# V stored by token of a block, then by block, in a block-sparse attention and feed-forward kernel

## The chip, the cores and the metric

The kernel is one program on one core of a Trainium2 chip. The core has a matrix engine (PE, with its weight loads shown as PEld), a vector engine (DVE), an activation engine (ACT), a general engine (POOL), and a queue engine (SP) that issues transfers. Transfers between DRAM and the on-chip memory (128 partitions) are carried out by 16 DMA engines. The metric is the device time of one execution in microseconds, median of several runs; lower is better.

## The reference

Attention with a block mask over 4 batches, 8 heads, 768 tokens and 64 values per head, and then a feed-forward layer with a softplus between two matrix products:

```python
block, n_blocks, n_rand = 32, 24, 3
mask = np.abs(blk_i - blk_j) <= 1
mask = mask | (blk_i == 0) | (blk_j == 0) | (blk_i == n_blocks - 1) | (blk_j == n_blocks - 1)
for qb in range(n_blocks):
    for kb in sampled_blocks[qb]:
        mask[qb * block:(qb + 1) * block, kb * block:(kb + 1) * block] = True
scores = np.where(mask, q @ k.T / sqrt(64), -1e9)
attn = softmax(scores)                 # attn / (sum + 1e-9)
x = (attn @ v), heads side by side     # 3072 tokens x 512
h = x @ w_in                           # 512 x 2048
out = softplus(h) @ w_out              # 2048 x 512
...
```

So a block of 32 queries sees its own block, the two beside it, the first and the last block, and three sampled ones: eight slots of 32 keys. The first and the last block of queries see all 24 blocks.

## The kernel before

**Sets of query blocks.** The 24 query blocks of a batch are taken in six groups `g` of four, in the order 1, 2, ..., 23, 0. Each group is a set, and the last group of a batch (blocks 21 and 22, 23 and 0) makes two: first a whole set (blocks 23 and 0, which see all keys), then a set of two blocks. That gives 7 sets for a batch and 28 in all. A set is worked off in two units (half of the heads each).

**The values of a set** lie in one of two buffers `vbuf` (`vg` in the trace), 128 partitions x 2 x 4 x 512 floats, that the sets use in turn. For a set of four blocks, `vd[0:96, 0, i]` holds the neighbour rows of block `i` (three blocks of 32 tokens on 96 partitions), `vd[96:128, 0, i]` and `vd[96:128, 1, i]` the first and the last block, and `vd[0:96, 1, i]` the three sampled blocks. `load_values(m)` loads them: one transfer from SP's queue for all neighbour rows (L549), transfers for the ends in the first two sets of a batch (L558, L561), and for each block a gather from POOL's queue with a table of row numbers (L567; L362 for the ends of the very first block). For a whole set three transfers (L542) bring all 768 rows of the batch.

**V in DRAM** is a table of 3072 rows (batch, then token) of 512 floats, 2 KB a row. So the rows of one block follow one another in DRAM, and the four neighbour rows that one partition takes (the same token of four blocks in a row) lie 64 KB apart. The pattern of L549 is written by `overlapping`:

```python
return bass.AP(at.tensor, at.offset, [pattern[0], [BLOCK * pattern[0][0], n], pattern[1]])
```

Its steps, outermost first, are 96 rows 2 KB apart, then `n` blocks, then the 512 floats of a row.

**The tables of row numbers** are made at the start: POOL writes the number of the token in its block on each partition (`io` L357, `first` L359), and DVE makes the row `block * 32 + token + batch * 768` of it (`ixf` L391, `ix` L396).

**What sets the order.** The work of the attention is cut into pieces (`pieces`: scores, values, transposes of a unit), and `attend` deals them out between the matrix products of the first feed-forward stage; between these `convert` runs the conversion of the weights (raw weights in at L148, converted ones parked in DRAM at L201). PE takes its instructions in that fixed order. SP's queue is in program order too. `value_piece` calls `values(n)` and, after the second unit of set `m`, `load_values(m + 2)`, since the buffer is free from then on. So the load of a set is issued when the set two before it is done, and it has to be there when PE comes to the first values of its own set. The keys of a batch (`kT`, L431) are loaded anew at the end of each batch.

After the attention, from about 430 us of the trace, the second feed-forward stage runs; it loads no values.

Of the kernel before, what the change touches and what calls it, by code (L numbers as in the profile page):

```python
# [15 lines left out]
ALU = mybir.AluOpType  # L16
# [3 lines left out]
BLOCK = 32  # L20
# [30 lines left out]
def sparse_attention_ffn(  # L51
# [22 lines left out]
    nc = tc.nc  # L74
    B, NG, P, NP, NI, _ = q.shape
    NB = k.shape[2]
    S = NB * BLOCK
    LAST = NB - 1
    NA = NP // 2
    NT, DM = out.shape  # L80
    NF = w_in.shape[0]
    NC = DM // P
    D = DM // (2 * NP)
    SCALE = 1.0 / float(D) ** 0.5
    NS = 8
    NR = 3
    TB = GROUPS * P
    NTB = NT // TB
    NCH = S // P
# [245 lines left out]
    rf = ac.tile([P, NB, NR], F32, name="rf")  # L335
# [3 lines left out]
    io = ac.tile([NR * BLOCK, 1], I32, name="io")  # L339
    first = ac.tile([P, 1], I32, name="first")  # L340
    iof = ac.tile([NR * BLOCK, 1], F32, name="iof")
    ixf = ac.tile([NR * BLOCK, NB], F32, name="ixf")
    ix = ac.tile([NR * BLOCK, B, NB], I32, name="ix")
# [8 lines left out]
    for i in range(NI):  # L352
        nc.gpsimd.iota(
            iu[i * BLOCK : (i + 1) * BLOCK], pattern=[[NI, NG]], base=1 + i, channel_multiplier=0
        )
    for s in range(NR):
        nc.gpsimd.iota(io[s * BLOCK : (s + 1) * BLOCK], pattern=[[0, 1]], base=0, channel_multiplier=1)  # L357
    for rows in (slice(0, NR * BLOCK), slice(NR * BLOCK, P)):
        nc.gpsimd.iota(first[rows], pattern=[[0, 1]], base=0, channel_multiplier=1)  # L359
    vbuf = [ac.tile([P, 2, NI, DM], F32, name=f"vg{n}") for n in range(2)]  # L360

    nc.gpsimd.indirect_dma_start(  # L362
        out=vbuf[0][:, 0, 0, :], out_offset=None, in_=v,
# [21 lines left out]
    def make_index():  # L385
        nc.vector.tensor_copy(out=iof, in_=io)
        nc.vector.tensor_copy(out=rf, in_=blk.rearrange("p (i s w) -> p i s w", s=NR, w=2)[:, :, :, 0])

        for s in range(NR):
            rows = slice(s * BLOCK, (s + 1) * BLOCK)  # L390
            nc.vector.tensor_scalar(  # L391
                out=ixf[rows], in0=rf[rows, :, s], scalar1=float(BLOCK), scalar2=iof[rows, 0:1],
                op0=ALU.mult, op1=ALU.add,
            )
        for b in range(B):
            nc.vector.tensor_scalar_add(out=ix[:, b], in0=ixf, scalar1=float(b * S))  # L396

    def make_mask():
        nc.vector.tensor_copy(out=iuf, in_=iu)
# [10 lines left out]
        nc.vector.tensor_single_scalar(out=hit, in_=tmp, scalar=1.0, op=ALU.is_le)  # L410
        for end in (0.0, float(LAST)):
            nc.vector.tensor_single_scalar(out=tmp, in_=rp, scalar=end, op=ALU.is_equal)
# [12 lines left out]
    kT, qc, vg = {}, {}, {}  # L425
# [7 lines left out]
    def load_kT(b, n, engine=nc.sync, parts=4):  # L433
        load_part(b, n * NB // parts, (n + 1) * NB // parts, engine)

    def overlapping(src, lo, n, rows):

        at = src[lo : lo + rows]
        pattern = [list(x) for x in at.ap]
        return bass.AP(at.tensor, at.offset, [pattern[0], [BLOCK * pattern[0][0], n], pattern[1]])  # L440

    def load_queries(m):
        if m >= len(order):
# [33 lines left out]
    def end_keys(m, copies):  # L477

        for copy, slot, blkno in zip(copies, (NR, 2 * NR + 1), (0, LAST)):
            copy(  # L480
# [4 lines left out]
    def gather_keys(m):  # L485
# [4 lines left out]
        def of_block(i):  # L490
# [15 lines left out]
            for s in range(NR):  # L506
                x = nc.s_assert_within(
                    eng.snap((r >> (16 * (i % 2) + 5 * s)) & 31), 0, LAST,
                    skip_runtime_bounds_check_because="a sampled block is one of the key blocks",
# [23 lines left out]
    def load_values(m):  # L533
        if m >= len(sets):
            return
        b, g, whole = sets[m]
        vd = vg[sets[m]] = vbuf[m % 2]
        if whole:
            rows = vd.rearrange("p c i f -> p (c i) f")
            for n in range(0, NCH, 2):  # L540
                lo = b * S + n * P
                nc.sync.dma_start(  # L542
                    out=rows[:, n : n + 2], in_=v[lo : lo + 2 * P].rearrange("(t p) f -> p t f", p=P)
                )
            return
        ni = NI if g < NG - 1 else 2

        i0 = 1 if m == 0 else 0
        nc.sync.dma_start(  # L549
            out=vd[0 : 3 * BLOCK, 0, i0:ni], in_=overlapping(v, b * S + (4 * g + i0) * BLOCK, ni - i0, 3 * BLOCK)  # L550
        )
        if g < 2:

            for c, lo in enumerate((b * S, (b + 1) * S - BLOCK)):
                i1 = i0 if c == 0 else 0
                if m < SPREAD:
                    if i1 == 0:
                        nc.sync.dma_start(out=vd[3 * BLOCK : P, c, 0], in_=v[lo : lo + BLOCK])  # L558
                    spread.append((vd[3 * BLOCK : P, c, 0:1], vd[3 * BLOCK : P, c, 1:]))
                    continue  # L560
                nc.sync.dma_start(  # L561
                    out=vd[3 * BLOCK : P, c, i1:],
                    in_=v[lo : lo + BLOCK].unsqueeze(1).to_broadcast([BLOCK, NI - i1, DM]),
                )

        def of_block(i):
            nc.gpsimd.indirect_dma_start(  # L567
                out=vd[0 : 3 * BLOCK, 1, i, :],
                out_offset=None,
                in_=v,  # L570
                in_offset=bass.IndirectOffsetOnAxis(ap=ix[:, b, 4 * g + 1 + i : 4 * g + 2 + i], axis=0),
            )

        value_work.extend((m, lambda i=i: of_block(i)) for i in range(ni))
# [6 lines left out]
    def scores(n):  # L581
        m, a = units[n]
        b, g, whole = sets[m]
        st = state[n]
        qd = qc[b, g]
        nmax = st["nmax"] = wk.tile([P, 2, 2], F32, tag="nmax", name=f"nmax{n}", bufs=4)
        st["pr"] = [wk.tile([P, S], F32, tag="pr", name=f"pr{n}_{r}", bufs=4) for r in range(2)]
        if not whole:
            gathered(key_work, place[b, g])
            kd = kg[place[b, g] % 2]  # L590
            ni = NI if g < NG - 1 else 2
            rows = slice(0, ni * BLOCK)
            ps = [ps_s.tile([P, 2, NS, BLOCK], F32, tag="s", name=f"s{n}_{r}") for r in range(2)]
            pr = [x[:, 0 : 2 * NS * BLOCK].rearrange("p (j s k) -> p j s k", j=2, s=NS) for x in st["pr"]]
            for j in range(2):
                p = 2 * a + j
                cols = slice(p * BLOCK, (p + 1) * BLOCK)
                for i in range(ni):
                    for r in range(2):
                        half = slice(64 * r, 64 * r + 64)  # L600
                        nc.tensor.matmul(  # L601
                            ps[r][32 * i : 32 * i + 32, j], qd[half, p, i, :], kd[half, i, :, cols],
                            start=True, stop=True,
                        )
            for r in range(2):
                for j in range(2):
                    nc.vector.tensor_tensor_reduce(  # L607
                        out=pr[r][rows, j], in0=ps[r][rows, j],
                        in1=mask[rows, g].unsqueeze(2).to_broadcast([ni * BLOCK, NS, BLOCK]),
                        scale=-SCALE, scalar=BIG, op0=ALU.add, op1=ALU.min,  # L610
                        accum_out=nmax[rows, r, j : j + 1],
                    )
            st["rows"] = ni * BLOCK
            st["chunks"] = 4
        else:

            pr = st["pr"]
            for t, (lo, hi) in enumerate(((0, NB // 2), (NB // 2, NB))):
                n_ = (hi - lo) * BLOCK
                ps = [ps_s.tile([P, 512], F32, tag="s", name=f"s{n}_{lo}_{r}") for r in range(2)]  # L620
                for o in range(2):
                    p = 2 * a + o
                    for r in range(2):
                        half = slice(64 * r, 64 * r + 64)
                        nc.tensor.matmul(  # L625
                            ps[r][64 * o : 64 * o + 64, 0:n_],
                            qd[half, p, 2:4, :].rearrange("p i q -> p (i q)"),
                            kT[b][half, lo:hi, p * BLOCK : (p + 1) * BLOCK],
                            start=True, stop=True,
                        )  # L630
                for r in range(2):
                    nc.vector.tensor_tensor_reduce(  # L632
                        out=pr[r][:, lo * BLOCK : hi * BLOCK], in0=ps[r][:, 0:n_],
                        in1=zero.to_broadcast([P, n_]),
                        scale=-SCALE, scalar=BIG, op0=ALU.add, op1=ALU.min, accum_out=nmax[:, r, t : t + 1],
                    )
            for r in range(2):
                nc.vector.tensor_tensor(out=nmax[:, r, 0:1], in0=nmax[:, r, 0:1], in1=nmax[:, r, 1:2], op=ALU.min)
            st["rows"] = P
            st["chunks"] = NCH  # L640
# [275 lines left out]
    for j in range(len(seq) + LEAD):  # L916
        if j >= SECOND:
            t, f = seq[j][1:] if j < len(seq) else (NTB, -1)
# [62 lines left out]
```

## Time and profile before

| | us |
|---|---|
| median of 3 runs | 831.7 |
| lowest, highest run | 827.58, 833.89 |
| span of the profiled execution (first to last instruction) | 812.1 |
| PE busy in the span | 781.7 |
| DVE, ACT, POOL busy in the span | 574.8, 489.6, 223.3 |

The profiled execution is one of its own; its time with what lies around its span is not among the three runs, and only its span is given. The median is 19.6 us above that span. Tables of the profile give the busy time of an engine, the granted clock of PE, the share of time for which the 16 DMA engines were busy on average, and the bytes that they moved per second. A packet is one piece that a DMA engine moves in one go. "Landing" is the time from issue to the arrival of the last byte. A transfer's KB are 1024 bytes, the MB of the queues are 10^6.

### The profile page before, as it was taken

What the parts mean: (1) busy time and instruction counts of PE and PEld (TensorE: products, weight loads), DVE (VectorE), ACT (ScalarE), POOL (GpSimd) and SP (SyncE); (2) the same over time, 40 slices, a digit from 0 to 9 for tenths busy, and PEclk for the clock granted to TensorE, in tenths of its full rate; (3) what the DMA queues carried; (4) which work ended last, traced back from release to release, by engine and by line L of the source; (5) the groups of instructions that cost most, each with busy time, mean ns of one, the idle gap of its engine ahead of it and who ended that gap; (6) DMA issues with size and microseconds to landing.
All of it is one profiled execution on the core that took longest, in us unless ns stands there. A gap on an engine that the chain in (4) does not pass through costs nothing.

```text
span 812.1 us, 21433 instructions
## 1 busy us (share of the span) xinstructions
PE 781.7 (96%) x8108; PEld 647.6 (80%) x8108; DVE 574.8 (71%) x1474; ACT 489.6 (60%) x1182; POOL 223.3 (27%) x389
## 2 busy tenths in 40 slices
PE   8878898999999999999999999999999999999997
PEld 8545676877677777778778988999988999988996
DVE  5778999876887777886655985656565656656564
ACT  5878785757767767767565764444444444444442
POOL 6864775635565436563000000000000000000000
PEclk9999898999999999999999999999999999999999
DMA  8899678687696777866425640304040312122021
GB/s 254 241 257 336 171 212 266 195 294 247 184 291 198 248 261 200 267 171 184 158 78 182 250 178 20 137 1 155 2 146 10 116 40 105 52 88 68 0 79 40
DMA packets 48408, 129.65 MB, mean 160 GB/s; under 512 B 5489, under 2 KB 5617, under 8 KB 46257
## 3 DMA queue, kind: packets, MB, share of 16 engines
q1 hardware_dynamic: 42304, 109.79, 42.3%
q0 software_dynamic: 5712, 17.57, 7.6%
q8 instruction: 64, 1.05, 0.5%
q10 hardware_dynamic: 288, 0.93, 0.3%
q14 instruction: 40, 0.32, 0.1%
HBM read 97.85 MB, written 30.41 MB: 158 GB/s over the span
## 4 chain that ended last, share of the span: by engine, by line
PE 82%; DVE 7%; ACT 6%; DMA 2%; issue 2%; POOL 0%; SPq 0%; ACTq 0%; DVEq 0%; POOLq 0%
PE o L295 11%; PE h L237 11%; PE o L297 10%; PE o L296 10%; PE h L238 10%; PE h L239 10%; PE s L601 5%; PE t L670 4%; PE x L700 4%; ACT pr L657 3%; PE warm L831 2%; DMA kT<-in_k_dram 1%; PE s L625 1%; DVE pr L607 1%; PE x L714 1%
## 5 line engine op out<-in xcount | busy, mean ns | idle before, releaser
L237 PE MATMUL h<-x,w 128*128 128x384 f32 x512 | 180.0, 352 | 0.4 <-DVE nmax L632 0.2
L238 PE MATMUL h<-x,w 128*128 128x384 f32 x512 | 173.7, 339 | 0.0
L239 PE MATMUL h<-x,w 128*128 128x384 f32 x512 | 173.1, 338 | 0.0
L250 DVE TENSOR_SCALAR u<-e 128x384 f32<-128x384 f32 x128 | 50.8, 397 | 155.8 <-ACT e L244 154.4
L295 PE MATMUL o<-w,gh 128*128 128x512 f32 x384 | 158.7, 413 | 0.0
L657 ACT ACTIVATE pr<-pr,nmax 128x256 f32<-128x256 f32 (+2 forms) x208 | 110.4, 532 | 74.6 <-DVE nmax L607 60.4
L297 PE MATMUL o<-w,gl 128*128 128x512 f32 x384 | 152.0, 396 | 1.2 <-issue 1.0
L296 PE MATMUL o<-w,gh 128*128 128x512 f32 x384 | 151.7, 395 | 0.0
L243 ACT ACTIVATE e<-h 128x384 f32<-128x384 f32 x128 | 62.4, 487 | 114.9 <-PE h L239 114.8
L267 ACT CAST gh<-u 128x384 fp32r<-128x384 f32 x128 | 65.6, 513 | 79.2 <-PE o L296 78.1
L237 PEld LDWEIGHTS h<-x,w 128*128 128x128 f32 x512 | 96.6, 189 | 19.4 <-issue 11.2
L567 POOL DMA_INDIRECT vg<-in_v_dram,ix x88 | 90.3, 1027 | 65.9 <-PE x L700 39.1
L238 PEld LDWEIGHTS h<-x,w 128*128 128x128 f32 x512 | 96.8, 189 | 6.5 <-issue 2.2
L511 POOL COPY kg<-kT 128x128 f32 x252 | 86.0, 389 | 41.2 <-PE s L601 38.8
L239 PEld LDWEIGHTS h<-x,w 128*128 128x128 f32 x512 | 96.6, 189 | 0.0
L295 PEld LDWEIGHTS o<-w,gh 128*128 128x128 f32 x384 | 72.0, 188 | 19.9 <-issue 7.1
L297 PEld LDWEIGHTS o<-w,gl 128*128 128x128 f32 x384 | 72.1, 188 | 18.8 <-issue 1.5
L296 PEld LDWEIGHTS o<-w,gh 128*128 128x128 f32 x384 | 72.2, 188 | 10.3 <-issue 0.4
L607 DVE CUSTOM_DVE_ANT_1 pr<-s,mask 128x256 f32<-128x256 f32 (+1 forms) x192 | 69.6, 414 | 14.5 <-PE s L601 14.5
L258 ACT ACTIVATE u<-u 128x384 f32<-128x384 f32 x128 | 66.9, 523 | 15.4 <-DVE e L252 15.2
L263 DVE TENSOR_TENSOR u<-u,e 128x384 f32<-128x384 f32 x128 | 73.6, 575 | 3.0 <-ACT u L258 2.4
L273 DVE TENSOR_TENSOR gl<-u,gh 128x384 fp32r<-128x384 f32 x128 | 73.0, 570 | 2.8 <-ACT gh L267 2.8
(81 smaller groups left out, 1088.6 us busy)
## 6 DMA issues: line engine op xcount, KB each, us to landing
vg<-in_v_dram SPq DMA_DIRECT2D x19, 768.0 KB, 5.8
xD<-x SPq DMA_DIRECT2D x8, 1536.0 KB, 7.4
x<-xD SPq DMA_DIRECT2D x8, 1536.0 KB
raw<-in_w_in_dram SPq DMA_DIRECT2D x16, 512.0 KB, 9.3
raw<-in_w_out_dram SPq DMA_DIRECT2D x16, 512.0 KB, 8.3
qc<-in_q_dram SPq DMA_DIRECT2D x24, 256.0 KB, 6.9
vg<-in_v_dram SPq DMA_DIRECT2D x12, 512.0 KB, 7.4
yD<-os SPq DMA_DIRECT2D x24, 256.0 KB, 2.5
```

Source lines behind the costliest of these rows:

```text
L237: nc.tensor.matmul(ph, wh[:, cols], hi[:, c], start=(c == 0), stop=False)
L238: nc.tensor.matmul(ph, wh[:, cols], lo[:, c], start=False, stop=False)
L239: nc.tensor.matmul(ph, wl[:, cols], hi[:, c], start=False, stop=(c == NC - 1))
L263: nc.vector.tensor_tensor(out=l, in0=l, in1=e, op=ALU.add)
L273: nc.vector.tensor_tensor(out=gl, in0=l, in1=G[n].bitcast(F32), op=ALU.subtract)
L295: nc.tensor.matmul(po[m], gh[:, cols], wh, start=first, stop=False)
L296: nc.tensor.matmul(po[m], gh[:, cols], wl, start=False, stop=False)
L297: nc.tensor.matmul(po[m], gl[:, cols], wh, start=False, stop=last)
L511: copy(out=kd[:, i, 1 + NR + s, :], in_=kT[b][:, bass.ds(x, 1), :].rearrange("p n f -> p (n f)"))
L567: nc.gpsimd.indirect_dma_start(out=vd[0 : 3 * BLOCK, 1, i, :], out_offset=None, in_=v, in_offset=bass.IndirectOffsetOnAxis(ap=ix[:, b, 4 * ...
L607: nc.vector.tensor_tensor_reduce(out=pr[r][rows, j], in0=ps[r][rows, j], in1=mask[rows, g].unsqueeze(2).to_broadcast([ni * BLOCK, NS, BLOCK]),
L657: nc.scalar.activation(x, x, AF.Exp, bias=nmax[rows, r, j : j + 1], scale=-1.0, accum_out=rs[rows, h : h + 1])
```

## The change

V is stored by batch, then by token of a block (32), then by block, with 25 places for the 24 blocks of a token (the last one is padding): row `(batch * 32 + token) * 25 + block`. The same token of successive blocks now lies in successive rows. A new function `tokens` writes the patterns of all loads of V. The neighbour load takes, on 96 partitions, one run of 8 KB (four rows); the whole set is one transfer with a run of 12 KB (six rows) on each of 128 partitions. For that, partition `s * 32 + token` of a whole set takes blocks `6 s` to `6 s + 5`, and the keys of its scores are read in the same order (`keys`). The tables of row numbers follow the new rows: POOL's numbers step by 25 from partition to partition, and the factor 32 of DVE's is gone. `first` gets its base by block.

```diff
+    PITCH = v.shape[0] // (B * BLOCK)
...
-    for s in range(NR):
-        nc.gpsimd.iota(io[s * BLOCK : (s + 1) * BLOCK], pattern=[[0, 1]], base=0, channel_multiplier=1)
-    for rows in (slice(0, NR * BLOCK), slice(NR * BLOCK, P)):
-        nc.gpsimd.iota(first[rows], pattern=[[0, 1]], base=0, channel_multiplier=1)
+    for s in range(NR + 1):
+        at = slice(s * BLOCK, (s + 1) * BLOCK)
+        if s < NR:
+            nc.gpsimd.iota(io[at], pattern=[[0, 1]], base=0, channel_multiplier=PITCH)
+        nc.gpsimd.iota(first[at], pattern=[[0, 1]], base=s % NR, channel_multiplier=PITCH)
...
-                out=ixf[rows], in0=rf[rows, :, s], scalar1=float(BLOCK), scalar2=iof[rows, 0:1],
-                op0=ALU.mult, op1=ALU.add,
+                out=ixf[rows], in0=rf[rows, :, s], scalar1=iof[rows, 0:1], scalar2=None, op0=ALU.add
...
-            nc.vector.tensor_scalar_add(out=ix[:, b], in0=ixf, scalar1=float(b * S))
+            nc.vector.tensor_scalar_add(out=ix[:, b], in0=ixf, scalar1=float(b * BLOCK * PITCH))
...
-    def overlapping(src, lo, n, rows):
-        at = src[lo : lo + rows]
-        pattern = [list(x) for x in at.ap]
-        return bass.AP(at.tensor, at.offset, [pattern[0], [BLOCK * pattern[0][0], n], pattern[1]])
+    def tokens(b, lo, n, parts=1, step=0):
+        at = v[b * BLOCK * PITCH + lo : b * BLOCK * PITCH + lo + 1]
+        row, one = [list(x) for x in at.ap]
+        pattern = [[PITCH * row[0], BLOCK], [row[0], n], one]
+        return bass.AP(at.tensor, at.offset, ([[step * row[0], parts]] if parts > 1 else []) + pattern)
...
-            for n in range(0, NCH, 2):
-                lo = b * S + n * P
-                nc.sync.dma_start(
-                    out=rows[:, n : n + 2], in_=v[lo : lo + 2 * P].rearrange("(t p) f -> p t f", p=P)
-                )
+            nc.sync.dma_start(out=rows[:, 0:NCH], in_=tokens(b, 0, NCH, NI, NCH))
...
-        nc.sync.dma_start(
-            out=vd[0 : 3 * BLOCK, 0, i0:ni], in_=overlapping(v, b * S + (4 * g + i0) * BLOCK, ni - i0, 3 * BLOCK)
-        )
+        nc.sync.dma_start(out=vd[0 : 3 * BLOCK, 0, i0:ni], in_=tokens(b, 4 * g + i0, ni - i0, 3, 1))
...
-            for c, lo in enumerate((b * S, (b + 1) * S - BLOCK)):
+            for c, end in enumerate((0, LAST)):
+                rows_v = tokens(b, end, 1)
...
+            keys = kT[b].rearrange("p (s c) f -> p c s f", s=NI)
...
-                            kT[b][half, lo:hi, p * BLOCK : (p + 1) * BLOCK],
+                            keys[half, lo:hi, :, p * BLOCK : (p + 1) * BLOCK],
```

Two places show how the instructions stand. On SP's queue around the first whole set (`vg` are value buffers, `raw` weights, `qc` queries, `kT` keys, `xD` a result parked in DRAM; behind the names stand partitions x counts of the written side), before:

```order
L148 DMA raw_1223<-in_w_in_dram 128x512
L542 DMA vg_174<-in_v_dram 128x2x512 x3
L447 DMA qc_0_1275<-in_q_dram 128x512
L148 DMA raw_1332<-in_w_out_dram 128x512
L431 DMA kT_1436<-in_k_dram 128x768 x4
L148 DMA raw_1456<-in_w_out_dram 128x512
L549 DMA vg_173<-in_v_dram 96x2x512
```

and with the change:

```order
L149 DMA raw_1225<-in_w_in_dram 128x512
L542 DMA vg_176<-in_v_dram 128x1x3072
L449 DMA qc_0_1275<-in_q_dram 128x512
L149 DMA raw_1332<-in_w_out_dram 128x512
L432 DMA kT_1436<-in_k_dram 128x768 x4
L149 DMA raw_1456<-in_w_out_dram 128x512
L547 DMA vg_175<-in_v_dram 96x1x1024
```

The three transfers of the whole set have become one and the counts of a partition one run; nothing has changed its place in the queue.

On POOL at the start of the program, before (`io` and `first` are the numbers from which the row tables are made):

```order
L353 IOTA iu 32x6 x3
L357 IOTA io 32x1 x3
L359 IOTA first 96x1
L359 IOTA first 32x1
L362 DMA vg_173<-in_v_dram,first 128x512
L567 DMA vg_173<-in_v_dram,ix 96x512 x4
```

and with the change:

```order
L354 IOTA iu 32x6 x3
L360 IOTA io 32x1
L361 IOTA first 32x1
L360 IOTA io 32x1
L361 IOTA first 32x1
L360 IOTA io 32x1
L361 IOTA first 32x1 x2
L364 DMA vg_175<-in_v_dram,first 128x512
L564 DMA vg_175<-in_v_dram,ix 96x512 x4
```

Two more IOTA instructions stand ahead of the first gather. On PE, DVE and ACT every instruction stands where it stood.

More of the change, by code (lines that the diff above doesn't have):

```diff
@@ L557, in load_values @@
                     if i1 == 0:
-                        nc.sync.dma_start(out=vd[3 * BLOCK : P, c, 0], in_=v[lo : lo + BLOCK])
+                        nc.sync.dma_start(out=vd[3 * BLOCK : P, c, 0:1], in_=rows_v)
                     spread.append((vd[3 * BLOCK : P, c, 0:1], vd[3 * BLOCK : P, c, 1:]))
@@ L562, in load_values @@
                     out=vd[3 * BLOCK : P, c, i1:],
-                    in_=v[lo : lo + BLOCK].unsqueeze(1).to_broadcast([BLOCK, NI - i1, DM]),
+                    in_=rows_v.to_broadcast([BLOCK, NI - i1, DM]),
                 )
@@ L617, in scores @@
             pr = st["pr"]
-            for t, (lo, hi) in enumerate(((0, NB // 2), (NB // 2, NB))):
-                n_ = (hi - lo) * BLOCK
+            keys = kT[b].rearrange("p (s c) f -> p c s f", s=NI)
+            for t, (lo, hi) in enumerate(((0, NCH // 2), (NCH // 2, NCH))):
+                n_ = (hi - lo) * P
                 ps = [ps_s.tile([P, 512], F32, tag="s", name=f"s{n}_{lo}_{r}") for r in range(2)]
@@ L632, in scores @@
                     nc.vector.tensor_tensor_reduce(
-                        out=pr[r][:, lo * BLOCK : hi * BLOCK], in0=ps[r][:, 0:n_],
+                        out=pr[r][:, lo * P : hi * P], in0=ps[r][:, 0:n_],
                         in1=zero.to_broadcast([P, n_]),
@@ L963 @@
         "k": k.reshape(B, NP, 2, NB, BLOCK, D).transpose(0, 2, 5, 3, 1, 4).reshape(B, 2 * D, NB, NP * BLOCK),
-        "v": v.transpose(0, 2, 1, 3).reshape(B * S, H * D),
+        "v": _np.pad(
+            v.reshape(B, H, NB, BLOCK, D).transpose(0, 3, 2, 1, 4), ((0, 0), (0, 0), (0, 1), (0, 0), (0, 0))
+        ).reshape(-1, H * D),
         "blocks": inputs["sampled_blocks"],
```

## The prediction

> **What bounds the kernel now.** I read the page's engine table first, then the 40 slices, then the chain that ended last.
>
> ```profile
> PE 781.7 (96%) x8108; PEld 647.6 (80%) x8108; DVE 574.8 (71%) x1474; ACT 489.6 (60%) x1182; POOL 223.3 (27%) x389
> PEclk9999898999999999999999999999999999999999
> DMA  8899678687696777866425640304040312122021
> ...
> PE 82%; DVE 7%; ACT 6%; DMA 2%; issue 2%; POOL 0%; SPq 0%; ACTq 0%; DVEq 0%; POOLq 0%
> ```
>
> PE is busy for 96% of the span at nearly full clock, and 82% of the last chain is PE work. DMA waits hold 2% of the chain, about 16 us. But the DMA row has its 6 to 9 tenths in the first 21 slices, which are the attention. The change touches only transfers of this stretch, so I read it by windows (columns: busy time of PE, PEld, DVE, ACT, POOL with counts; granted clock, mean DMA share, GB/s), with two later windows as prices.
>
> ```profile
> 0.00:429.00 429.00, 402.79 (x6207) 306.87 (x6209) 333.13 (x980) 303.38 (x802) 223.30 (x389) 0.98 0.74 223
> 140.00:180.00 40.00, 40.00 (x645) 31.29 (x645) 31.63 (x93) 29.22 (x81) 20.18 (x31) 1.00 0.71 226
> 380.00:429.00 49.00, 48.79 (x688) 37.93 (x689) 29.63 (x95) 30.84 (x80) 2.31 (x3) 1.00 0.35 122
> 435.00:445.00 10.00, 10.00 (x52) 9.01 (x51) 5.78 (x12) 5.31 (x12) 0.00 (x0) 1.00 0.99 353
> 505.00:515.00 10.00, 10.00 (x51) 8.91 (x51) 4.96 (x11) 4.93 (x10) 0.00 (x0) 1.00 0.42 157
> ```
>
> In the 429 us of attention the average DMA engine is busy for 0.74 x 429 = 317 us, and while busy it moves 223 / (0.74 x 16) = 18.8 GB/s. The windows at 435 (rows of 2 KB, weights) and 505 (runs of 12 KB, one `x` load) give 22.3 and 23.4 GB/s for one engine with little beside it. So PE bounds the stretch, with some 110 us of slack on each DMA engine, as long as the sixteen share the load.
>
> How they share it can be counted on ACT's queue:
>
> ```profile
> q1 hardware_dynamic: 42304, 109.79, 42.3%
> ...
> q10 hardware_dynamic: 288, 0.93, 0.3%
> ...
> kT<-in_k_dram ACTq DMA_DIRECT2D x1, 832.0 KB, 10.2
> ...
> blk<-in_blocks_dram ACTq DMA_DIRECT2D x1, 72.0 KB, 5.6
> ```
>
> Two transfers of 128 runs each make 256 packets; the queue counts 288. The 32 more are sixteen closing packets for each, one for every engine that took part. A run of 6.5 KB (832 KB / 128) is one packet: the runs are moved as the pattern lists them and not cut again.
>
> **The change part by part.** First the loads from SP's queue, with the time from issue to landing in the last column:
>
> ```profile
> vg<-in_v_dram SPq DMA_DIRECT2D x19, 768.0 KB, 5.8
> ...
> vg<-in_v_dram SPq DMA_DIRECT2D x12, 512.0 KB, 7.4
> ...
> vg<-in_v_dram SPq DMA_DIRECT2D x4, 384.0 KB, 8.1
> ...
> vg<-in_v_dram SPq DMA_DIRECT2D x1, 576.0 KB
> ```
>
> The 24 neighbour loads are 19 x 768 + 4 x 384 + 576 = 16,704 KB, the four whole sets 12 x 512 = 6,144 KB: together 23.4 MB of the 95.7 MB (223 GB/s x 429 us) of the stretch.
>
> *Longer runs.* 2 KB becomes 8 or 12 KB. By the rows at 435 and 505 a busy engine goes from 22.3 to 23.4 GB/s, which for 23.4 / 16 = 1.46 MB an engine saves 3 us of engine time in the whole kernel. That is nearly nothing.
>
> *The outermost step.* Before, the source pattern of a neighbour load began with 96 rows, that of a whole part with 128; sixteen equal shares can be taken from either. Now the source begins with `[step * row, parts]`: 3 for a neighbour load, 4 for a whole set, while the written side still begins with 96 or 128 partitions. What has to be decided is whether a transfer is divided along the outermost step of its patterns. If so, only 3 or 4 shares come out, on three or four engines. No row shows a transfer whose outer count is under sixteen: those of the value loads and of ACT's queue are 32, 96 and 128. I take the division along the outermost step, since the packet count shows patterns executed as written, run by run, with nothing that cuts them anew.
>
> [...]
>
> The price: three engines carry 16,704 / 3 + 6,144 / 4 = 7,104 KB, or 7.27 MB, of values each; at 23.4 GB/s (the row for long runs) that is 311 us. Their sixteenth of before falls away: 1.46 MB at 18.8 GB/s, 78 us. So each of these engines has 317 - 78 + 311 = 550 us of work for a stretch of 429 us, 121 us too much. In the last 49 us nothing overflows: 0.35 x 49 = 17 us, plus 16 for a whole set and a half-size load, leave 16 us idle. That makes +137 us. Against it stands that the other traffic may run faster when thirteen engines have less to do: its 239 us at 18.8 GB/s are 202 us at the 22.3 of the row at 435, which takes off 37 us and gives +100. Between these I take the middle, **+118 us**.
>
> Does it reach PE? One period of two sets, on PE and on SP's queue (start, duration):
>
> ```profile
> 143.99 1.10 PE L700 MATMUL x<-vg,pt 128*32 128x64 f32 x64
> 151.96 1.10 PE L700 MATMUL x<-vg,pt 128*32 128x64 f32 x64
> 159.49 1.10 PE L700 MATMUL x<-vg,pt 128*32 128x64 f32 x64
> 167.46 1.10 PE L700 MATMUL x<-vg,pt 128*32 128x64 f32 x64
> ...
> 145.04 0.33 SPq L549 DMA_DIRECT2D vg<-in_v_dram  x1
> ...
> 160.54 0.33 SPq L549 DMA_DIRECT2D vg<-in_v_dram  x1
> ```
>
> A set takes 15.5 us. The load issued at 145.04, right behind the last values of its buffer, is needed at 167.46: 22.4 us of cover. A neighbour load on three engines takes 262 KB at 23.4 GB/s, 11.2 us instead of 2.6 us (49 KB at 18.8), so alone it would still be covered. But it isn't alone: by the row at 140 a period holds 0.71 x 15.5 = 11.0 us of other and own work, and 11.0 + 8.6 = 19.6 us don't fit into 15.5. The backlog grows with every set, and from then on PE waits at the first values (L700) of a set, with everything behind them in its fixed order, the feed-forward products too. SP's queue carries queries, weights and keys behind the value loads, so these come late as well. For a whole set the cover is the time from issue to need here:
>
> ```profile
> 62.07 1.51 SPq L542 DMA_DIRECT2D vg<-in_v_dram  x3
> ...
> 82.30 1.62 PE L714 MATMUL x<-vg,pt 128*64 128x64 f32 x48
> ```
>
> 20.2 us, against 16.8 us on four engines (393 KB) plus the other work of that time.
>
> *Three transfers into one* takes two issues of 0.5 us (1.51 / 3) off SP, hidden under its waits. *Gathers.* The rows of a gathered block lie 51,200 B apart instead of 2,048. The nearest row is the long strided key load above (128 runs, 12 KB apart in the table, 10.2 us for 832 KB, in the crowded start), which shows no penalty: I take 0, with the range left to hold a few us either way. *The start.*
>
> ```profile
> 2.00 0.47 POOL L357 IOTA io<- 32x1 int32 x3
> 2.54 0.30 POOL L359 IOTA first<- 96x1 int32 x2
> 3.13 1.13 POOL L362 DMA_INDIRECT vg<-in_v_dram,first  x1 [0.29 <-POOL first L359]
> 7.82 0.91 POOL L567 DMA_INDIRECT vg<-in_v_dram,ix  x1 [3.56 <-DVE ix L396]
> ```
>
> Two more IOTAs are 2 x 0.15 = 0.3 us ahead of the first gather; the next one waits 3.56 us for the table from DVE anyway, which hides it (uncovered: 0.3 us). DVE's `ixf` loses one of two operations in three tiny instructions: 0. *Scores of a whole set* (L625) read the keys as 3 x 4 runs of 32 instead of 12; same columns, on PE. Their total is 2% of PE's time at most, as the row shows; I take 0.
>
> ```profile
> L625 PE MATMUL s<-kT,qc 64*64 64x384 f32 x128 | 16.4, 499 | 1.3 <-DVE nmax L632 1.3
> ```
>
> **The sum.** 812.1 + 118 = 930 us of span. The three runs (827.58 to 833.89) have their median 19.6 us above the profiled span, which I keep: 950 us.
>
> Ends of this case: if the four whole loads stay covered (4 x (16.8 - 5.2) = 46 us less) and the other traffic is quick, +54 us, 885. If at each of three new batches the keys, on the chain for up to 7.47 us now, wait behind one whole load more (3 x 16.8 us) on top of +137, +187 us, 1019.
>
> ```profile
> 36.04 8.66 DMA vg<-in_v_dram,ix
> ...
> 74.28 3.10 DMA kT<-in_k_dram
> ...
> 190.44 7.47 DMA kT<-in_k_dram
> ```
>
> **The rivals.** *Spread as before.* The transfers are divided by partitions, whatever the source's outer step, and all sixteen engines carry them. For it: so they did in every transfer of the trace. Against it: each of those could be divided along its outermost step too. Then only the longer runs are left, 3 us an engine under a stretch that PE bounds: 828 to 833 us, no change. It decides if the queue's closing packets stay sixteen for a value load. *Spread, and waits on the chain shrink.* The three DMA waits above are 19.2 us; shorter queues might take half of the first and of the last, 8 us: 823 us, faster by 1%. Against it: two of the three are for keys, one for a gather, and none for a load that the change makes longer in its runs. *Confined, but hidden.* Three engines, and the period holds it nevertheless, since a load has 22.4 us of cover: 832 us. It decides below 15.5 - 11.2 = 4.3 us of other work in a period; the row at 140 gives 11.0 - 2.6 = 8.4, or 7 us at 22.3 GB/s. *Gathers slowed* by the far rows would add to any case: a gather waited for at 36.04 for 8.66 us, doubled, costs some 9 us once, 841 us, slower by 1%.
>
> **How the numbers follow.** Confined and not hidden: 0.87. Spread, no change: 0.07; confined but hidden: 0.02; spread and faster: 0.03; spread with slowed gathers: 0.01. A measurement of this kernel tells about 1% from no change. So slower 0.88, same 0.09, faster 0.03. The time is that of the first case, 950. Its own range, 885 to 1019, holds most of its 0.87; I widen it to 875 to 1025 for the gathers and the start, which leaves out the unchanged cases near 830 and little else.
>
> **What would show it.** Right: SP's queue q1 has 42,304 - (19 x 384 + 288 + 4 x 192) - 3,072 + (24 x 96 + 4 x 128) packets of runs, and closing packets of 24 x 3 + 4 x 4 in place of 36 x 16, in all 33,208 (33,568 if value loads keep sixteen). Landing of a 768 KB load is 13 us or more instead of 5.8, of a whole set 18 or more. The mean DMA share of the attention falls while the stretch grows to about 545 us, and PE's largest wait is L700 or L714 for `vg<-in_v_dram`. The second stage keeps its 382 us. Wrong: a landing near 6 us, an attention that ends near 430 us, or PE waiting for keys or gathers alone.

## The result and the profile after

| | before | after |
|---|---|---|
| median, us | 831.0 | 976.38 |
| lowest to highest of 4 runs each, us | 827.58 to 833.89 | 975.33 to 984.78 |
| span of the profiled execution, us | 812.1 | 975.3 |

The ratio is 1.1765, with a 95% interval of 1.1719 to 1.1811: the changed kernel is slower by 18%. The profiled execution of after took 977.25 us. On another chip the same pair gave 1.1681 (1.1608 to 1.1754). The kernel before has medians of 811 to 833 us on the chips that were used, so the experiments are told in ratios to the runs of before on their own chip.

The two spans can't be compared like the medians. In every run the time is about 2 us above the span (after: 977.25 and 975.3). So the profiled execution before, with its span of 812.1 us, took some 814 us. That is less than any run of before in this table and fits the quicker chips; which chip it ran on is not known. The spans are 163 us apart, but the medians on one chip 145 us (976.38 - 831.0), and 141 us on the other chip (974.85 - 833.46, run e8 below). What the change costs is read from the medians.

The page of after: busy time of the engines with their share of the span, the granted clock and the DMA share in 40 slices, SP's queue, and the chain that ended last by engine and by line.

```profile
PE 816.0 (84%) x8108; PEld 670.9 (69%) x8108; DVE 571.4 (59%) x1474; ACT 491.0 (50%) x1182; POOL 220.1 (23%) x391
PEclk9676767999879899879899989999999999999999
DMA  6374574656574655663645315721130212213010
...
q1 hardware_dynamic: 33208, 109.79, 34.4%
...
PE 58%; DMA 36%; ACT 2%; issue 2%; DVE 2%; SPq 0%; DVEq 0%; ACTq 0%
DMA qc<-in_q_dram 18%; DMA vg<-in_v_dram 11%; PE h L238 8%; PE o L296 8%; PE h L239 8%; PE h L240 8%; PE o L297 8%; PE o L298 8%; DMA kT<-in_k_dram 7%; PE s L598 3%; PE x L698 3%; PE t L668 2%; PE s L623 2%; PE x L712 1%; PE y L743 1%
```

DMA had 2% of the chain and now has 36%, while the mean DMA share of the attention fell from 0.74 to 0.53. The packets of SP's queue are 33,208, the number worked out for three and four closing packets. With sixteen for each value load they would be 33,568.

The windows of after, the attention (its last values are taken at 592.6 us), the second stage, and seven quiet microseconds in which no engine works and PE waits for a load:

```profile
0.00:592.60 592.60, 437.53 (x6223) 330.62 (x6223) 329.84 (x982) 304.69 (x802) 220.10 (x391) 0.84 0.53 162
592.60:975.30 382.70, 378.49 (x1891) 340.31 (x1885) 241.53 (x493) 186.35 (x380) 0.00 (x0) 1.00 0.25 89
68.00:75.00 7.00, 0.00 (x0) 0.00 (x0) 0.00 (x0) 0.00 (x0) 0.00 (x0) 0.50 0.19 66
```

The second stage takes 382.7 us, and 812.1 - 429.0 = 383.1 us before. So the whole loss lies in the attention. How long the attention takes on one and the same chip, the products with the values of two runs below show, e5 (which costs what the kernel before does) and e8 (the change once more). The range behind the durations is that of their starts:

```profile
L699 PE MATMUL x<-vg,pt x2816: 216/219/316, 21.1 to 444.8; 128*32 128x64 f32 x188
L698 PE MATMUL x<-vg,pt x2816: 216/219/317, 33.9 to 593.0; 128*32 128x64 f32 x188
```

It ends at 444.8 us without the loss and at 593.0 us with it; the 429 us of the trace before are some 16 us too short to compare with, most likely those of a quicker chip. The row at 68 shows how the loss comes about: 0.19 x 16 = 3.0 engines are at work, and these move 66 / 3.04 = 21.7 GB/s each.

Which load PE waits for, in the chain (start, duration), and one such place on SP's queue and on PE:

```profile
48.33 27.14 DMA qc<-in_q_dram
...
85.12 24.69 DMA qc<-in_q_dram
...
123.16 20.43 DMA kT<-in_k_dram
...
176.96 21.79 DMA vg<-in_v_dram
198.76 23.12 DMA qc<-in_q_dram
```

```profile
47.54 0.75 SPq L547 DMA_DIRECT2D vg<-in_v_dram  x1
48.33 0.45 SPq L449 DMA_DIRECT2D qc<-in_q_dram  x1
```

```profile
75.61 2.26 PE L598 MATMUL s<-kg,qc 64*32 64x256 f32 x32 [17.05 <-DMA qc<-in_q_dram]
```

A query load of 256 KB, issued right behind a neighbour load, lands after 27 us; before, its median was 6.9 us. PE stands at the scores that need it for 17 us. The queries have less cover than the value load in front of them, as the trace before shows for the pair issued at 145 us:

```profile
145.42 0.47 SPq L447 DMA_DIRECT2D qc<-in_q_dram  x1
...
164.05 1.09 PE L601 MATMUL s<-kg,qc 64*32 64x256 f32 x32
```

These queries are those of the set after the one whose values are loaded, and scores run two units ahead of values. So they are needed after 18.6 us, the values after 22.4 us, and the queries are missed first. PE's waits in after (us in total, times, longest):

```profile
PE s L598 <- ACT pt L675: 55.5, 5, 19.1
PE s L598 <- DMA qc<-in_q_dram: 47.6, 9, 17.1
PE s L623 <- DMA qc<-in_q_dram: 16.1, 4, 8.7
...
PE x L712 <- DMA vg<-in_v_dram: 4.1, 1, 4.1
```

The page puts the first row down to a copy on ACT. But its three long waits (19.1, 17.5 and 17.8 us, one at each new batch) all end 2.2 us after a wait for keys in the chain, such as the one at 123.16: it is the keys that came last. So PE itself waits 64 us for queries, some 54 us for keys, and 4 us for values.

### The profile page after: what moved, and what is told of

Its sections match the earlier page's. It is cut to its first block, busy times and chain, and to the rows that moved or that the text cites. A ratio compares the mean times of both kernels' runs of the same rounds, so it can differ in the third digit from the quotient of the medians.

```text
span 975.3 us, 21418 instructions
## 1 busy us (share of the span) xinstructions
PE 816.0 (84%) x8108; PEld 670.9 (69%) x8108; DVE 571.4 (59%) x1474; ACT 491.0 (50%) x1182; POOL 220.1 (23%) x391
## 3 DMA queue, kind: packets, MB, share of 16 engines
q1 hardware_dynamic: 33208, 109.79, 34.4%
## 4 chain that ended last, share of the span: by engine, by line
PE 58%; DMA 36%; ACT 2%; issue 2%; DVE 2%; SPq 0%; DVEq 0%; ACTq 0%
DMA qc<-in_q_dram 18%; DMA vg<-in_v_dram 11%; PE h L238 8%; PE o L296 8%; PE h L239 8%; PE h L240 8%; PE o L297 8%; PE o L298 8%; DMA kT<-in_k_dram 7%; PE s L598 3%; PE x L698 3%; PE t L668 2%; PE s L623 2%; PE x L712 1%; PE y L743 1%
## 5 line engine op out<-in xcount | busy, mean ns | idle before, releaser
L238 PE MATMUL h<-x,w 128*128 128x384 f32 x512 | 183.0, 357 | 2.3 <-DVE e L254 2.0
L239 PE MATMUL h<-x,w 128*128 128x384 f32 x512 | 176.5, 345 | 0.0
L240 PE MATMUL h<-x,w 128*128 128x384 f32 x512 | 175.6, 343 | 0.0
L296 PE MATMUL o<-w,gh 128*128 128x512 f32 x384 | 161.5, 420 | 0.0
L598 PE MATMUL s<-kg,qc 64*32 64x256 f32 x1408 | 67.3, 446 | 105.7 <-ACT pt L675 55.5
L297 PE MATMUL o<-w,gh 128*128 128x512 f32 x384 | 153.8, 400 | 0.0
L251 DVE TENSOR_SCALAR u<-e 128x384 f32<-128x384 f32 x128 | 46.8, 366 | 162.2 <-ACT e L245 162.2
L598 PEld LDWEIGHTS s<-kg,qc 64*32 64x32 f32 x1408 | 29.5, 118 | 128.4 <-issue 119.0
L238 PEld LDWEIGHTS h<-x,w 128*128 128x128 f32 x512 | 98.4, 192 | 24.2 <-issue 12.8
L564 POOL DMA_INDIRECT vg<-in_v_dram,ix x88 | 87.1, 990 | 77.5 <-PE x L698 51.8
L239 PEld LDWEIGHTS h<-x,w 128*128 128x128 f32 x512 | 98.9, 193 | 8.1 <-issue 3.8
L240 PEld LDWEIGHTS h<-x,w 128*128 128x128 f32 x512 | 98.7, 193 | 0.1
L296 PEld LDWEIGHTS o<-w,gh 128*128 128x128 f32 x384 | 73.1, 190 | 21.5 <-issue 8.8
L297 PEld LDWEIGHTS o<-w,gh 128*128 128x128 f32 x384 | 73.7, 192 | 10.5 <-issue 0.6
```

Of the source, the lines that this page charges most:

```text
L238: nc.tensor.matmul(ph, wh[:, cols], hi[:, c], start=(c == 0), stop=False)
L239: nc.tensor.matmul(ph, wh[:, cols], lo[:, c], start=False, stop=False)
L240: nc.tensor.matmul(ph, wl[:, cols], hi[:, c], start=False, stop=(c == NC - 1))
L296: nc.tensor.matmul(po[m], gh[:, cols], wh, start=first, stop=False)
L297: nc.tensor.matmul(po[m], gh[:, cols], wl, start=False, stop=False)
L564: nc.gpsimd.indirect_dma_start(out=vd[0 : 3 * BLOCK, 1, i, :], out_offset=None, in_=v, in_offset=bass.IndirectOffsetOnAxis(ap=ix[:, b, 4 * ...
```

## The experiments

Theory A: a transfer is divided along the outermost step of its patterns, and the few engines that carry it make the loss. Rivals: the layout itself costs (gathered rows far apart, padded pitch, long runs); or the loss is a matter of the order in the queue and not of work on the engines.

### All value loads on sixteen engines by splitting (e1, e2, e3)

```diff
-        nc.sync.dma_start(out=vd[0 : 3 * BLOCK, 0, i0:ni], in_=tokens(b, 4 * g + i0, ni - i0, 3, 1))
+        for s in range(3):
+            nc.sync.dma_start(out=vd[s * BLOCK : (s + 1) * BLOCK, 0, i0:ni], in_=tokens(b, 4 * g + i0 + s, ni - i0))
...
-            nc.sync.dma_start(out=rows[:, 0:NCH], in_=tokens(b, 0, NCH, NI, NCH))
+            for s in range(NI):
+                nc.sync.dma_start(out=rows[s * BLOCK : (s + 1) * BLOCK, 0:NCH], in_=tokens(b, s * NCH, NCH))
```

> The changed layout, table and runs stay; each neighbour load becomes three transfers of 32 partitions, each whole set four, so that every source pattern begins with 32 rows. Theory A (a transfer is divided along its outermost step, and the three or four busy engines make the loss): the loss goes away, 826 to 838 us, q1's closing packets are sixteen for each value load. Theory B (the layout itself costs: gathered rows 51,200 B apart, padded pitch, long runs): 950 us or more, as the change. A mixture would lie between.

> Only the neighbour loads are split into three transfers of 32 partitions; the four whole sets stay single transfers whose source begins with 4. Theory A: at most 4 x (16.8 - 5.2) = 46 us of work more on four engines than before, much of it within the slack of the stretch: 832 to 865 us. If each whole load stalls what is queued behind it in full: about 880.

> Only the whole sets are split into four transfers of 32 partitions; the neighbour loads stay single transfers whose source begins with 3. Theory A, as work of an engine: 317 - 57 + 244 to 270 (5.70 MB at 23.4 to 21.1 GB/s) = 504 to 530 us for a stretch of 429: 910 to 950 us.

Measured: both split (e1) 1.077 (1.072 to 1.082), neighbours alone (e2) 1.100 (1.097 to 1.104), whole sets alone (e3) 1.133 (1.129 to 1.137). (The 21.1 GB/s at one end of what was expected for e3 stands in no row of a profile; the quiet row above gives 21.7.) In e1 more than half of the loss is gone, but 7.7% stay, which theory A had not said. The chain that ended last in e1, by engine, has 4% of DMA waits where after has 36%, so little of what stays is a wait for a load:

```profile
PE 71%; DVE 12%; ACT 9%; DMA 4%; issue 3%; POOLq 0%; POOL 0%; SPq 0%; DVEq 0%; ACTq 0%
```

The split had a second effect that I had not looked for. With more transfers in the program, the scheduler set instructions on PE, DVE and ACT in another order: when PE's matrix products are taken together where neighbours are alike, 257 of 1,148 such groups of after stand elsewhere in the trace of e1. So these three runs can't tell order from layout, and e9 and e5 were made for that.

### The old layout in the order of e1, and the split alone (e9, e6)

The kernel before, its neighbour loads split in the same way, and in e9 its whole sets too:

```diff
-        nc.sync.dma_start(
-            out=vd[0 : 3 * BLOCK, 0, i0:ni], in_=overlapping(v, b * S + (4 * g + i0) * BLOCK, ni - i0, 3 * BLOCK)
-        )
+        for s in range(3):
+            nc.sync.dma_start(
+                out=vd[s * BLOCK : (s + 1) * BLOCK, 0, i0:ni],
+                in_=overlapping(v, b * S + (4 * g + i0 + s) * BLOCK, ni - i0, BLOCK),
+            )
...
+            for s in range(NI):
+                nc.sync.dma_start(
+                    out=rows[s * BLOCK : (s + 1) * BLOCK, 0:NCH],
+                    in_=v[b * S : (b + 1) * S].rearrange("(c p) f -> p c f", p=P)[s * BLOCK : (s + 1) * BLOCK],
+                )
```

> The kernel before with its old layout and 2 KB runs, each neighbour load as three transfers of 32 partitions and each whole set as four: instruction for instruction the order of the run with all sixteen (e1), which split transfers had moved on PE, DVE and ACT. Theory A (the 1.077 of that run comes from the moved order and the many transfers): 1.05 to 1.09. Theory B (it comes from long runs written to only 32 partitions by sixteen engines): 1.00 to 1.02.

> The kernel before with its old layout and 2 KB runs, but each neighbour load as three transfers of 32 partitions. Theory A (the 1.077 of the run with all sixteen comes from the splitting: 32 partitions for each transfer, and three transfers for one in SP's queue): 1.03 to 1.09. Theory B (it comes from the layout): 1.00.

Measured: e9 1.060 (1.053 to 1.067), e6 1.006 (1.004 to 1.008). With the old layout and 2 KB runs, in the order of e1, most of e1's 7.7% is there too. So it belongs to the splitting and the order that came of it; which of the two costs how much, no run separates. Splitting the neighbour loads alone costs 0.6%, though it moves 120 of PE's 1,148 groups; the rest comes with the split whole sets. The 1.7 points between e9 and e1 stay open: they were measured on two chips, and in microseconds e1 takes less time than e9 (873.65 against 880.68).

### The same transfers with the tokens outermost (e5)

```diff
-        return bass.AP(at.tensor, at.offset, ([[step * row[0], parts]] if parts > 1 else []) + pattern)
+        part = [[step * row[0], parts]] if parts > 1 else []
+        return bass.AP(at.tensor, at.offset, pattern[:1] + part + pattern[1:])
```

> The change with its two value patterns written with the 32 tokens as the outermost step and the 3 or 4 parts inside: one transfer as before, the same bytes and runs to the same 96 or 128 partitions. The rows land on partition 3 t + s (or 4 t + s) instead of 32 s + t, so the values of the attention are mixed up; no other work changes. Theory A (the outermost step divides a transfer; the rest of the layout costs nothing): 1.00 of the kernel before (0.99 to 1.01), sixteen closing packets for each value load. Theory B (what is left in the run with all sixteen, 1.077, is the layout: far gathered rows, padded pitch, long runs): 1.06 to 1.09.

Measured: 1.0004 (0.9969 to 1.0039). On every engine the order is that of the changed kernel. The engine line and SP's queue on the page of e5:

```profile
PE 790.5 (96%) x8108; PEld 651.2 (79%) x8108; DVE 571.9 (69%) x1474; ACT 488.7 (59%) x1182; POOL 225.6 (27%) x391
...
q1 hardware_dynamic: 33568, 109.79, 41.4%
```

The packets are those of sixteen closing packets a load, and PE is busy for 96% as before. Only the order of two steps in a pattern differs from the changed kernel: the whole 17 to 18% hang on it. (The rows land on other partitions, so this run is a measurement and no kernel to use. No run here has the long runs, sixteen engines and the right values in one transfer.) It also shows what the longer runs are worth here, with a quarter or less of the packets: nothing that can be measured.

### The gathers alone (e7)

```diff
     v: bass.AP,
+    v2: bass.AP,
...
-                in_=v,
+                in_=v2,
```

(`v2` is a second copy of V in the new layout, and the tables of row numbers are those of the changed kernel.)

> The kernel before, with a second copy of V in the new layout from which the sampled blocks are gathered (rows 51,200 B apart); all loads from SP's queue as before. Theory A: 1.00 (0.99 to 1.01). Theory B (far gathered rows cost): 1.02 to 1.07, with a landing of the gathers above the 7.8 us of before.

Measured: 1.0011 (0.9987 to 1.0035). Here is the queue of the gathers in the kernel before and in e7 (packets, MB, share of the engines):

```profile
q0 software_dynamic: 5712, 17.57, 7.6%
```

```profile
q0 software_dynamic: 5712, 17.57, 7.3%
```

That is 62 us of 812.1 and 61 us of 830.6 on each engine: rows that are 51,200 B apart are gathered here as quickly as neighbouring ones.

### The old layout with one step turned (e12)

```diff
-        return bass.AP(at.tensor, at.offset, [pattern[0], [BLOCK * pattern[0][0], n], pattern[1]])
+        return bass.AP(at.tensor, at.offset, [[BLOCK * pattern[0][0], n], pattern[0], pattern[1]])
```

> The kernel before, old layout and old table, with one thing turned: the source pattern of the neighbour loads counts the four blocks outermost and the 96 rows inside (so rows land permuted and the values are mixed up). Nothing else moves on any engine. Theory A (outermost step): four engines for a load (three in the first, two in the half-size ones), 5.70 MB x 3/4 = 4.3 MB on the first four, 183 to 204 us of work instead of 57: 317 - 57 + 183 to 204 = 443 to 464 us for a stretch of 429 us, 1.03 to 1.09, and a landing of 10 us or more. Theory B (the division follows the partitions of the written side): 1.00.

Measured: 1.055 (1.050 to 1.060), in the middle of what the engines' work gave.

SP's queue in e12 (packets, MB, share of the engines):

```profile
q1 hardware_dynamic: 35959, 109.79, 38.3%
```

and PE's largest wait (us in total, times, longest):

```profile
PE s L601 <- DMA qc<-in_q_dram: 19.8, 4, 10.7
```

The packets give the engines that took part. The written side now has one run on each of 96 partitions, 24 x 96 packets for the 8,352 of before, and 42,304 - 8,352 + 2,304 - 24 x 16 + (19 x 4 + 3 + 4 x 2) = 35,959: four engines for four blocks, three for three, two for two. So the loss needs neither the new layout nor long reads from DRAM. And PE's wait is for the queries behind the neighbour load, as in after.

### One part confined at a time (e10, e11)

`tokens` of e5 for one of the two patterns only:

```diff
-        return bass.AP(at.tensor, at.offset, ([[step * row[0], parts]] if parts > 1 else []) + pattern)
+        part = [[step * row[0], parts]] if parts > 1 else []
+        lead = pattern[:1] if parts == NI else []
+        return bass.AP(at.tensor, at.offset, lead + part + pattern[len(lead):])
```

(e11 has `NR` for `NI`.)

> The change, with only the whole sets' pattern turned (32 tokens outermost; their rows land on permuted partitions, so those values are mixed up); neighbour loads still begin with 3. The order on all engines is that of the change. As work of an engine: 317 - 57 + 244 to 270 = 504 to 530 us for the stretch of 429: 1.09 to 1.14 of before.

> The change, with only the neighbour loads' pattern turned (32 tokens outermost; their rows land on permuted partitions, so those values are mixed up); whole sets still begin with 4. If each of the four loads stalls PE by what it takes longer than its cover of 20.2 us leaves (16.8 us alone, beside 11 us of other work): 4 x 5 to 4 x 12 us, 1.02 to 1.06 of before. If the cover holds: 1.00.

Measured: neighbours on three 1.103 (1.096 to 1.110), as the engines' work gave; whole sets on four 1.102 (1.093 to 1.111), well above what was expected. SP's queue has 33,256 packets in e10 and 33,520 in e11, so the closing packets give three and four engines for each kind of load by itself. By work alone four engines have time left there: 317 - 21 + 67 = 363 us for 429, an estimate from 6.29 MB of whole sets at 18.8 GB/s on sixteen engines and at 23.4 on four. Here are SP's queue in e11 around the first whole set (start, duration), the chain there, and two of PE's largest waits (total, times, longest):

```profile
69.72 0.67 SPq L544 DMA_DIRECT2D vg<-in_v_dram  x1
...
81.77 1.75 SPq L432 DMA_DIRECT2D kT<-in_k_dram  x4
```

```profile
81.77 28.95 DMA kT<-in_k_dram
```

```profile
PE s L600 <- ACT pt L677: 75.8, 7, 27.7
...
PE x L714 <- DMA vg<-in_v_dram: 10.3, 1, 10.3
```

The keys of the next batch, issued 12 us behind the whole load, hold up the chain for 28.95 us; before, the first such wait was 3.10 us and another 7.47. Nothing covers them, since their buffer becomes free only when the last scores of the old batch are done. (The page puts PE's waits of up to 27.7 us down to a copy on ACT, of `pt`; that copy was long done, and what came last was the keys.) 75.8 + 10.3 = 86 us is the size of the loss (915.56 - 831.92 = 84 us). Why the keys take so long is shown in part only. In this window of e11 PE is nearly idle, and yet the mean DMA share is full:

```profile
85.00:95.00 10.00, 0.29 (x3) 0.05 (x1) 0.00 (x0) 0.00 (x0) 3.52 (x4) 0.64 1.03 163
```

There an engine moves 163 / (1.03 x 16) = 9.9 GB/s, less than half of the 21.7 above, and by the mean share that is not four engines alone; what slows the others stays open. The two parts add up to 1.205, more than the 1.17 to 1.18 of both. Where one has already stopped PE, the other may cost less; no run shows this by itself. A ratio also depends on the chip: e3 has three engines for the neighbour loads as e10 has, and takes 919.15 us against 917.1, but on a quicker chip, where that is 1.133.

### Queries ahead of the values (e4), and the change again (e8)

```diff
-                if ended[2] is not None:
-                    load_values(ended[2] + 2)
+                late = ended[2]
+            else:
+                late = None
             if scored is not None:
                 load_queries(scored + 2)
+            if late is not None:
+                load_values(late + 2)
```

> The change as it is, but on SP's queue the query load of a set is issued ahead of the value load instead of behind it (same transfers, same engines). Theory C (the loss is a matter of latency: queries, with a shorter cover than the values, wait behind a slow load in the same queue, while the three engines have time left): the query waits, 18% of the last chain, go, and the time falls under 900 us. Theory D (the three engines are simply full for the whole stretch): the wait moves to another load, 955 to 990 us.

> The change as it is, for a ratio on the same chip and in the same call as the others: 1.17 to 1.21.

Measured: e4 973.12 us (971.17 to 977.81), and the change itself 974.85 us in e8 and 976.38 in the first runs. (Against its own chip's before e4 is 1.201, e8 1.168. Those chips differ for the kernel before, 810.66 and 833.46 us. The change itself was not run on e4's chip; that chips hardly differ for kernels that wait for DMA is what e3 and e10 suggest, with 919.15 and 917.1 us on two chips.) PE's largest waits in e4 (us in total, times, longest), the first put down to a copy on ACT, though at a new batch it is the keys that come last, as in e11:

```profile
PE s L598 <- ACT pt L675: 69.2, 7, 24.2
PE x L698 <- DMA vg<-in_v_dram: 56.6, 18, 11.2
```

The queries are no longer waited for, the values are, and the time is far from the 900 us of theory C. For the changed kernel as a whole the engines' work decides (theory D), and the order in the queue only who is late.

## Why the prediction was right, and where it was off

**Three and four engines.** Right, and shown in four ways: the packets of after (33,208, where e5 has 33,568), the DMA share of a quiet stretch (0.19, three of sixteen), the time without the small outer count (1.0004 in e5), and the time with such a count in the old layout (1.055 in e12). The packets of e12 (35,959) are those of two, three and four engines for outer counts of two, three and four. Before the result only the packet count on ACT's queue (288 for 256 runs) spoke for this, and that fits a division by partitions as well; the 0.87 was the author's estimate. Which of the sixteen engines they are, no run here shows. So none shows either that the three of a neighbour load are among the four of a whole set, as the 16,704 / 3 + 6,144 / 4 KB of the prediction and the first four engines of the expectation for e12 take them. What the runs show is the time of each kind of load on its few engines, 1.103 (e10) and 1.102 (e11), and of both, 1.168 (e8) and 1.1765.

**The size.** 950 us were forecast, 976 measured; against the 831 us of before that is +118 (950 less the 831.7 us known then) and +145. Two terms were off, in opposite directions.

The first is the middle between +137 and +100. The +100 took for granted that the other traffic speeds up to 22.3 GB/s, from 239 to 202 us on each engine. It did not. In after the engines are busy for 0.53 x 592.6 = 314 us on average, 5,025 us for all sixteen; the 23.4 MB of values take 23.4 MB / 21.7 = 1,078 us of that, and 247 us an engine are left for the rest. And the three engines moved the values at 21.7 GB/s in the quiet row, not 23.4. With this rate, without a speed-up and with the three engines again among the four, the same sum is 7.27 MB / 21.7 = 335 us, 317 - 78 + 335 = 574 us of work, and with the 16 us idle at its end an attention of 590 us; 592.6 was measured. Against the 444.8 us of e5 that is +145, as the medians have it. That it comes so near is agreement of a sum, an estimate from rows, and not proof of each stall.

The second is the 19.6 us that the prediction added for what lies around the span. No run shows them: time and span differ by about 2 us, and the rest was the difference of the profiled execution before from this chip's runs. The sum of work above reaches the measured attention without any such addition. The 19.6 us made up for part of what the first term lacked: of the span the forecast was 930 us, and 975.3 came. That the time came within 26 us is in part luck.

**Where PE waits.** Half right. The prediction put the largest wait at the values (L700, L714), and said that queries, weights and keys behind the value loads come late as well. In after it is these that stop PE: 64 us for queries and some 54 for keys against 4 us for values. (The chain has 18% for queries, 11% for values and 7% for keys, and in e8, the same kernel, 14%, 15% and 7%: these shares change from run to run.) The step that failed reads the cover from the value load alone, 22.4 us; the queries behind it in the same queue have 18.6. e4 shows that the order did not decide the time. The landing of the value loads, which the prediction named as a sign, has no figure in after's page.

**Whole sets.** The prediction priced them at 46 us of extra work that might stay covered, and named the keys behind them only for the upper end. Alone they cost 10%, by the keys' wait (e11).

**What was costed at nothing.** Longer runs, three transfers into one, the IOTAs, the order of the keys in the scores of a whole set: together 1.0004 in e5. The gathers: 1.0011 in e7. The second stage: 382.7 us, 383.1 before.

**The rivals.** *Spread as before* gave its time exactly, but for another kernel: it is what e5 does. *Spread with shorter waits* (823 us) is not seen in e5. *Confined, but hidden* fell with the result, as the row at 140 us had it. *Gathers slowed* fell with e7.

## What to carry to other kernels

Read the source pattern of a transfer outermost step first: here a count of 3 or 4 in front left three or four DMA engines to carry everything (33,208 packets for 33,568, and 0.19 x 16 = 3.0 engines at work in the quiet stretch), although 96 or 128 partitions were written. Long contiguous runs were no gain here: 1.1765 with the small count that their pattern put in front, 1.0004 without it. Count packets: here the closing packets of a transfer told how many engines took part (33,208 in after, 33,568 in e5, 35,959 in e12). Ask of a slow transfer what stands behind it in its queue: the queries, with 18.6 us of cover against 22.4 us of the values, were missed first, and PE waited 64 us for a load that the change never touched. And before a trace serves as the base of a sum, hold its span against the runs: here it was some 17 us short of them, and that difference was added to the forecast as if it were a cost.

## What the runs showed of the hardware that was not expected

**The clock of an idle PE.** In the row of after at 68 us, with PE idle for all of the 7 us, the granted clock is 0.50. What lower clocks add is seen in the attention of e5 and e8, which ran on one chip and have the same order on PE:

```profile
0.00:445.00 445.00, 412.10 (x6224) 310.87 (x6224) 330.74 (x982) 302.73 (x802) 225.65 (x391) 0.97 0.71 215
0.00:593.20 593.20, 431.81 (x6224) 324.19 (x6224) 326.75 (x982) 303.75 (x802) 221.79 (x391) 0.86 0.53 161
```

The same matrix products take 431.8 us of PE time in e8 instead of 412.1, at a granted clock of 0.86 instead of 0.97. So of the 148 us between these two executions only 128 are more idle time (161.4 and 32.9), and 20 are slower work.

**Transfers move instructions on engines that never see them.** Splitting loads, with no other edit, set 257 of PE's 1,148 groups of matrix products elsewhere (e1), and the split kernel e9, which has the same order, lost 6% (1.060). An experiment on a transfer has to be compared with a kernel in the same order.
